# Full-array products for the scores and the edges of an attention, and two copies moved to ScalarE

## The chip, the cores and the metric

The kernel runs on one core of one Trainium2 chip. A core has five engines that run at the same time, each through its own list of instructions in order: TensorE (PE: matrix products; PEld is its weight load), VectorE (DVE), ScalarE (ACT), GpSimd (POOL) and SyncE (SP), which here issues the DMAs. They meet at semaphores only. The metric is the device time in microseconds (us). Lower is better.

## The reference

An attention over 4 batches and 12 heads of 448 rows of 64 numbers, with RMS-normed queries and keys, feeds two expert layers:

```
q_n, k_n = rmsnorm(q, g_q), rmsnorm(k, g_k)
scores = q_n @ k_n.T / sqrt(64); attn = softmax(scores); out = attn @ v
x = out as 1792 x 768
h = x @ w_in;  x = (h * sigmoid(h)) @ w_out              # moe, d_ff 2048
h = x @ w_in;  y = (h * sigmoid(1.702 h)) @ w_out        # moe2
```

All is float32. A float32 operand is kept as two float32r parts, a high part `xh` and a low part `xl = x - xh`, and a product is the sum of three: low by high, high by low, high by high.

## The kernel before

**Attention.** 48 heads are taken as 24 pairs (`NP`). A pair's 448 rows are three chunks of 128 (`NK` = 3) and an edge of 64 rows (`HP`); the edges of the two heads of a pair stand together in one tile of 128 partitions, so a pair has `NG` = 7 groups of rows. On the partitions of `qh`, `ql`, `kh` and `kl` (64 numbers of each head) the first head has 0 to 63 and the second 64 to 127.

What one pair does, by function: `load_qk`, `load_qt`, `load_v` (SP) bring q and k by rows, q already transposed, and v. `square`, `rms_fold`, `polish`, `k_norm` (POOL), `rms_sum` (DVE) and `rms_exp` (ACT) make the norms. `k_T` transposes k on TensorE (L426 for the chunks, `halves` L417 for the edge); `k_hi` (ACT) and `k_lo` (DVE) split it. `q_hi` (DVE, L461) and `q_lo` (POOL, L466) split the transposed q; `v_hi` (DVE, L491) and `v_lo` (POOL, L498) split v. `stack_q` and `stack_k` copy, by DMA, high and low parts on top of each other, so that one product over 128 partitions gives two of the three terms.

`s_mm` makes the scores of one chunk for both heads: the third term, `ql` by `kh`, as two products of 64 partitions, one for each head (L529), then two stacked ones of 128 (L533). The edge of both heads is one group of three products of 128 (L510). The first two pairs take another way (L521). `s_max` (DVE), `s_bias` (POOL) and `s_exp` (ACT) make the softmax. `a_T` transposes the exponentials on TensorE; its last part (m = 6) has the edge's keys (L593, then `halves`). `a_hi` (ACT) and `a_lo` (DVE) split them; `pv` multiplies by v (L631, L624). `recip` (DVE), `r_wide` (ACT), `r_T` (TensorE: L578, `halves`) and `r_copy` (ACT) spread the reciprocal sums, and `x_mul` (DVE) multiplies them in.

`halves` makes the edge's 128 x 64 block into 64 x 64 for each head: two products whose results are 64 partitions high and stand above each other. Each appears as two instructions in the trace.

**Order.** Each step has an offset in `OFF`, in units of an eighth of a pair's turn (`STEP` = 8): `put(STEP * p + OFF[name], ...)`. The tasks are sorted by that number and recorded in that order, so `OFF` alone sets what stands where on each engine. Tiles come from pools with few buffers: four PSUM tiles for scores, two for `a_T`, one for `k_T` and `r_T` together, two buffers for `ql`, `qs`, `ks`, `v`.

From pair 14 on, work for the experts runs in between: `w_conv` turns the 64-bit words of the weights into float32 (ACT, DVE), `w_sum`, `s_hi`, `s_lo` make sums and parts of the weights, and `t_sum`, `t_hi`, `t_lo` sums and parts of the attention's result. All of `t_sum`, `t_lo`, `w_sum` and `s_lo` of this stretch stand on POOL.

**Experts.** 32 units, each seven products of nine instructions (L795, in the order 1, 6, 2, 7, 5, 4, 3), gates, and eight output groups (L904). The first product 4 of a unit waits for a DVE sum (`u`, L888).

Of the kernel before, what the change touches and what calls it, by code (L numbers as in the profile page):

```python
# [75 lines left out]
    "load_qt": -24.5,  # L76
    "load_v": -19.56,
# [4 lines left out]
    "k_norm": -17.87,  # L82
    "k_T": -17.84,
    "k_hi": -16.72,
    "k_lo": -15.3,
    "stack_k": -12.87,
    "q_hi": -17.59,
    "stack_q": -16.68,
    "q_lo": -15.56,
    "v_hi": -6.13,  # L90
    "v_lo": -5.1,
    "s_mm": [-10.89, -7.19, -6.56, -4.96],
    "s_max": [-8.72, -8.6, -6.81, -6.6, -5.38, -4.86, -3.22],
    "s_bias": [-8.32, -6.49, -3.93, -2.94],
    "s_exp": [-7.99, -6.67, -4.87, -3.93, -3.05, -1.3, -1.65],
    "a_T": [-0.76, 1.15, 1.43, 2.5, 3.55, 5.1, 5.94],
    "a_hi": [-0.57, 1.72, 1.87, 4.31, 5.3, 6.24, 7.08],
    "a_lo": [1.02, 2.19, 3.18, 4.6, 5.84, 6.72, 7.86],
    "pv": [2.33, 4.68, 7.7, 9.04],
    "guard": -0.37,  # L100
    "recip": -0.12,
    "r_T": 2.13,
    "r_copy": 3.56,
    "x_mul": 9.46,
    "square": [-24.61, -23.96],
    "lead": [-0.92, 3.78],
    "r_wide": 1.49,
    "w_in": [-51.94, -46.87, -42.73, -40.66, -38.6, -36.0, -33.79, -32.28],
    "w_sum": [-27.36, -26.93, -23.43, -20.47],
    "s_hi": [-30.21, -23.39, -21.4, -18.46],  # L110
    "s_lo": [-28.76, -17.66, -16.28, -14.05],
    "w_out": [-31.16, -25.15, -24.76, -19.09, -18.66, -16.19, -14.68, -10.2],
    "switch": -4.9,
    "t_step": 4.05,
    "t_hi": {1: -79.5, 2: -74.41, 6: -4.77, 7: -1.79, 5: -0.02, 4: 5.6, 3: 5.46},
    "t_lo": {1: -78.66, 2: -72.86, 6: -4.18, 7: 2.3, 5: 2.91, 4: 9.05, 3: 8.34},
    "t_sum": {5: -85.04, 6: -65.06, 7: -56.34, 4: -53.67},
    "second": [-18.32, -15.3, -15.0, -9.57, -14.27, -9.18, -7.33, -6.76],
}
# [3 lines left out]
def kernel(  # L123
# [206 lines left out]
    def attention():  # L330
        st = ExitStack()
        with st:
# [62 lines left out]
            def polish(p):  # L395
                ms, y = rs[p]
                w = sp.tile([128, 2, NG], F32, tag="w", name="w")
# [9 lines left out]
            def k_norm(p):  # L407
                n = raw.pop(p)[:, 1]
                nc.gpsimd.tensor_tensor(
                    n, n,  # L410
                    rs[p][1][:, 1].unsqueeze(2).to_broadcast([128, NG, D]), op=ALU.mult
                )
                kn[p] = n

            def halves(ps, src):
                for i in range(2):
                    nc.tensor.matmul(  # L417
                        ps[64 * i:64 * i + 64, NK * 128:S], src, ident[:, 64 * i:64 * i + 64],
                        start=True, stop=True,
                    )  # L420

            def k_T(p):
                ps = ps_t.tile([128, 512], F32, tag="t", name="t")
                n = kn.pop(p)
                for c in range(NK):
# [4 lines left out]
                halves(ps, n[:, 2 * NK])  # L430
# [48 lines left out]
            def v_parts(t, pad):  # L479
# [7 lines left out]
                return main, t[:, NK * w:]  # L487
# [12 lines left out]
            def s_mm(p, c):  # L500
# [6 lines left out]
                if c == NK:  # L507
                    edge = slice(NK * 128, NK * 128 + 128)
                    for n, (x, y) in enumerate(((1, 0), (0, 1), (0, 0))):
                        nc.tensor.matmul(  # L510
                            ps[0], qq[p][x][:, edge], kk[p][y], start=(n == 0), stop=(n == 2)
                        )
                    return
                chunk = slice(128 * c, 128 * c + 128)
                if p < 2:
                    spans = (((0, 0, S),), ((HP, 0, S - HP), (0, S - HP, HP)))
                    for n, (x, y) in enumerate(((1, 0), (0, 1), (0, 0))):
                        for i in range(2):
                            a = slice(64 * i, 64 * i + 64)
                            for d0, s0, w in spans[i]:  # L520
                                nc.tensor.matmul(  # L521
                                    ps[i][:, d0:d0 + w], qq[p][x][a, chunk],
# [4 lines left out]
                for i in range(2):  # L527
                    a = slice(64 * i, 64 * i + 64)
                    nc.tensor.matmul(  # L529
                        ps[i], qq[p][1][a, chunk], ks[p][a, i], start=True, stop=False  # L530
                    )
                for i in range(2):
                    nc.tensor.matmul(  # L533
                        ps[i], qs[p][:, i, chunk], ks[p][:, i], start=False, stop=True
                    )
# [6 lines left out]
            def s_bias(p, c):  # L542
# [3 lines left out]
                    rr[p][:, 1, g], rr[p][:, 0, g], rs[p][1][:, 0, g], op=ALU.mult  # L546
                )

            def s_exp(p, m):
# [3 lines left out]
                else:  # L553
# [5 lines left out]
                    out=o, in_=sps.pop((p, m)), func=ACTF.Exp, scale=rs[p][1][:, 0, g],  # L559
# [9 lines left out]
            def r_wide(p):  # L569
                rw[p] = ap.tile([128, NG, D], F32, tag="rw", name="rw", bufs=1)  # L570
                nc.scalar.copy(rw[p], rr.pop(p)[:, 3].unsqueeze(2).to_broadcast([128, NG, D]))

            def r_T(p):
                ps = ps_t.tile([128, 512], F32, tag="t", name="t")
                w = rw.pop(p).rearrange("p g d -> p (g d)")
# [3 lines left out]
                halves(ps, w[:, 128 * NK:])  # L579
# [6 lines left out]
            def a_T(p, m):  # L586
# [4 lines left out]
                if m == 2 * NK:  # L591
# [6 lines left out]
                    halves(ps, ec[p][:, NK * 128:])  # L598
# [20 lines left out]
            def pv(p, j):  # L619
                if j == 0:  # L620
                    xps[p] = ps_x.tile([128, S], F32, tag="x", name="x")
                for n, (y, z) in enumerate(((1, 0), (0, 0), (0, 1))):
                    if j == NK:
                        nc.tensor.matmul(  # L624
                            xps[p], vv[p][y][:, 3 * NK * D:], at[p, 2 * NK][z],
# [22 lines left out]
            vbuf = []  # L648
            for i in range(2):
                vbuf.append([  # L650
                    late.tile([128, DM], F32R, tag=f"v{nm}{i}", name=f"v{nm}{i}")[:, :(3 * NK + 2) * D]
                    for nm in "hl"
                ])
                for w in vbuf[i]:
                    nc.gpsimd.memset(f32(w), 0.0)
# [354 lines left out]
```

## Time and profile before

| what | us |
|---|---|
| median of three runs | 1248.39 (1246.15 to 1253.01) |
| the profiled execution's own time | 1250.27 |
| its span, first to last instruction | 1248.5 |
| TensorE busy | 1214.1 (97%) |
| DVE, ACT, POOL busy | 952.0, 659.1, 541.8 |
| attention | up to about 339.5 |
| mean granted TensorE clock | 0.996 |

How to read it: the profile's busy shares are means over the whole span. The attention and the experts load the engines in other ways, so the rows further down are taken from single stretches. A line such as L529 is a line of the kernel before. The granted clock is 1.00 at 2.4 GHz and 0.50 at 1.2 GHz.

### The profile page before, as it was taken

To read this page: it belongs to the slowest core of one execution; us is meant where nothing else is said; L and a number is where in the kernel's file an instruction comes from. 1 tells how busy PE (TensorE), PEld (TensorE's weight loads), DVE (VectorE), ACT (ScalarE), POOL (GpSimd) and SP (SyncE) were. 2 spreads that over 40 slices of the span, in tenths; PEclk is the share of its full clock that TensorE was granted. 3 is DMA by queue.
4 is the path that set the end of the run, shared out by engine and by line. 5 is a ranking of instruction groups with operands and counts; after the bars stand their busy time and mean duration, and the time that the engine had idled before them with its cause. 6 is when DMAs were issued, how large, how long until landed. Compare 5 with 4: busy or idle time off the path is not lost.

```text
span 1248.5 us, 17966 instructions
## 1 busy us (share of the span) xinstructions
PE 1214.1 (97%) x6294; PEld 1059.6 (85%) x6294; DVE 952.0 (76%) x1358; ACT 659.1 (53%) x1270; POOL 541.8 (43%) x677
## 2 busy tenths in 40 slices
PE   5999999999999999999999999899999999999998
PEld 4777777777888888888888888799999989999997
DVE  7888888898678999988788998846666573555563
ACT  4778888877864444454444445553333354333332
POOL 6676679988532224434222332622233242222221
PEclk9999999999999999999999999999999999999999
DMA  4655554465144455533666766122121131111112
GB/s 142 178 147 145 145 150 143 133 198 152 39 152 152 156 182 171 175 114 103 213 228 212 242 225 207 51 89 90 64 74 53 38 129 62 51 51 57 58 38 89
DMA packets 66123, 159.13 MB, mean 127 GB/s; under 512 B 11504, under 2 KB 29424, under 8 KB 66032
## 3 DMA queue, kind: packets, MB, share of 16 engines
q1 hardware_dynamic: 66032, 157.98, 39.9%
q8 instruction: 50, 0.82, 0.3%
q14 instruction: 41, 0.34, 0.1%
HBM read 108.53 MB, written 30.67 MB: 111 GB/s over the span
## 4 chain that ended last, share of the span: by engine, by line
PE 73%; DVE 13%; POOL 5%; issue 3%; ACT 3%; DMA 2%; DVEq 0%; SPq 0%; POOLq 0%; ACTq 0%
PE o L904 33%; PE h L795 23%; PE x L631 5%; PE a L605 3%; PE s L533 2%; DVE ol L285 2%; DVE r L229 2%; PE s L529 1%; POOL gl L812 1%; DVE r L538 1%; POOL acc L316 1%; DVE tl L323 1%; PE t L426 1%; PE a L603 1%; PE x L624 1%
## 5 line engine op out<-in xcount | busy, mean ns | idle before, releaser
L812 POOL TENSOR_TENSOR gl<-g,gh 128x448 fp32r<-128x448 f32 x96 | 118.0, 1229 | 501.4 <-ACT gh L811 500.5
L904 PE MATMUL o<-gl,oh 128*128 128x448 f32 x768 | 282.8, 368 | 3.5 <-POOL gl L812 3.3
L904 PE MATMUL o<-gh,ol 128*128 128x448 f32 x768 | 281.5, 367 | 2.9 <-DVE acc L912 2.5
L904 PE MATMUL o<-gh,oh 128*128 128x448 f32 x768 | 280.6, 365 | 0.0
L795 PE MATMUL h<-th,sl 128*128 128x448 f32 x672 | 175.7, 370 | 5.1 <-DVE u L888 3.8
L795 PE MATMUL h<-tl,sh 128*128 128x448 f32 x672 | 175.1, 369 | 0.0
L795 PE MATMUL h<-th,sh 128*128 128x448 f32 x672 | 174.6, 368 | 0.0
L904 PEld LDWEIGHTS o<-gl,oh 128*128 128x128 f32 x768 | 144.2, 188 | 22.8 <-POOL gl L812 9.5
L904 PEld LDWEIGHTS o<-gh,ol 128*128 128x128 f32 x768 | 144.3, 188 | 17.1 <-DVE acc L912 1.9
L904 PEld LDWEIGHTS o<-gh,oh 128*128 128x128 f32 x768 | 144.2, 188 | 11.6
L916 DVE SCALAR_TENSOR_TENSOR acc<-o,acc 128x896 f32<-128x896 f32 x84 | 91.6, 1091 | 73.8 <-PE o L904 73.6
L795 PEld LDWEIGHTS h<-th,sl 128*128 128x128 f32 x672 | 125.1, 188 | 20.8 <-DVE u L888 8.6
L795 PEld LDWEIGHTS h<-th,sh 128*128 128x128 f32 x672 | 126.7, 189 | 11.9
L795 PEld LDWEIGHTS h<-tl,sh 128*128 128x128 f32 x672 | 126.7, 188 | 11.3
L616 DVE TENSOR_TENSOR al<-a,ah 128x448 fp32r<-128x448 f32 x168 | 103.9, 619 | 36.1 <-ACT ah L612 33.9
L808 ACT ACTIVATE g<-c 128x448 f32<-128x448 f32 x96 | 55.6, 579 | 118.5 <-DVE c L891 117.5
L884 ACT COPY m<-h 128x448 f32<-128x448 f32 x32 | 17.0, 533 | 177.3 <-PE h L795 177.3
L558 ACT ACTIVATE e<-s,r,y 128x448 f32<-128x448 f32 x144 | 104.2, 726 | 10.9 <-POOL r L545 7.1
L612 ACT CAST ah<-a 128x448 fp32r<-128x448 f32 x168 | 87.4, 534 | 42.4 <-PE a L605 29.0
L538 DVE TENSOR_REDUCE r<-s 128x1 f32<-128x448 f32 x168 | 97.5, 614 | 5.7 <-PE s L533 3.7
L912 DVE TENSOR_TENSOR acc<-o,acc 128x896 f32<-128x896 f32 x84 | 90.9, 1083 | 9.0 <-PE o L904 8.9
L888 DVE TENSOR_TENSOR u<-h,m 128x448 f32<-128x448 f32 x64 | 39.8, 622 | 71.6 <-PE h L795 71.0
(135 smaller groups left out, 2206.7 us busy)
## 6 DMA issues: line engine op xcount, KB each, us to landing
d<-w SPq DMA_DIRECT2D x88, 384.0 KB, 3.5
r<-in_moe_w_in SPq DMA_DIRECT2D x32, 768.0 KB, 4.5
r<-in_moe_w_out SPq DMA_DIRECT2D x32, 768.0 KB, 4.7
w<-d SPq DMA_DIRECT2D x32, 384.0 KB, 2.6
w<-r SPq DMA_DIRECT2D x32, 384.0 KB, 3.0
qk<-in_qk SPq DMA_DIRECT2D x22, 448.0 KB, 3.4
qs<-qh SPq DMA_DIRECT2D x88, 96.0 KB, 2.2
qt<-in_q_t SPq DMA_DIRECT2D x24, 256.0 KB, 3.2
```

The lines of the kernel that those rows point to most:

```text
L538: nc.vector.tensor_reduce(rr[p][:, 0, m:m + 1], sps[p, m], axis=AX.X, op=ALU.max, negate=True)
L558: nc.scalar.activation(out=o, in_=sps.pop((p, m)), func=ACTF.Exp, scale=rs[p][1][:, 0, g], bias=rr[p][:, 1, g], accum_out=rr[p][:, 2, g],)
L612: nc.scalar.copy(at[p, m][0], aps[p, m])
L616: nc.vector.tensor_tensor(w, aps.pop((p, m)), f32(at[p, m][0]), op=ALU.subtract)
L631: nc.tensor.matmul(xps[p], vv[p][y][:, c0:c0 + 2 * D], at[p, 2 * j + i][z], start=(j == 0 and n == 0 and i == 0), stop=False,)
L795: nc.tensor.matmul(ps, w[:, c0:c0 + 128], x[:, kk], start=(start and c == 0), stop=(c == 3 * KH - 1), skip_group_check=True,)
L808: nc.scalar.activation(out=g, in_=src, func=ACTF.Silu, scale=(1.0 if first else BETA2))
L812: engine(ENGINE["gate"][key]).tensor_tensor(gl, g, gh.bitcast(F32), op=ALU.subtract)
L888: nc.vector.tensor_tensor(u2 if i == 6 else u3, b, m1, op=ALU.add)
L904: nc.tensor.matmul(o[:, i], x[:, ms], y, start=(t == 0 and c == 0), stop=(t == 1 and c == 2),)
L912: nc.vector.tensor_tensor(a, o, a, op=ALU.add)
L916: nc.vector.scalar_tensor_tensor(a, o, 1.0 / BETA2, a, op0=ALU.mult, op1=ALU.add)
```

## The change

- **Scores.** `q_lo` writes the low part of each head into a tile of its own head, `qlow`, whose other 64 partitions are zero (set once at the start). The third term of the scores then is a product of 128 partitions against the stacked `ks`, as the others. The four products of a chunk go head by head.
- **Edges.** A tile `wide` (128 x 128, zero but for two 64 x 64 blocks) takes the edge's block, written by two DVE copies (`r_edge`, `e_edge`); one product with `twice` (two identities of 64 above each other, in a spare part of a v tile) folds it (`folded`). There is one `wide` for both uses. k's edge is laid out with zeros from the host, so that `k_T` takes it by a fourth transpose; the tiles of the norms have 15 groups for 14.
- **Engines.** `q_hi` and `v_hi` go from DVE to ACT, but for the first pair. Of the three instructions of `q_lo` one is on DVE and two on POOL. Some `t_lo`, `t_sum`, `w_sum`, `s_lo` before the experts go from POOL to DVE.
- **Order.** `OFF` has new numbers throughout; on SP, `load_qk` now stands ahead of `load_v`, and `stack_q` right ahead of `stack_k`.

```diff
     "load_qk": -26.52,
-    "load_qt": -24.5,
+    "load_qt": -20.29,
...
-    "s_mm": [-10.89, -7.19, -6.56, -4.96],
+    "s_mm": [-10.89, -7.63, -6.88, -5.33],
...
+    "hi_on": ["p", "p"],
+    "q_lo_on": ["v", "p", "p"],
+    "edge_on": ["v", "v"],
+    "t_lo_on": {1: "p", 2: "v", 6: "v", 7: "p", 5: "p", 4: "v", 3: "v"},
+    "t_sum_on": {5: "v", 6: "v", 7: "p", 4: "v"},
+    "w_sum_on": ["p", "v", "p", "p"],
+    "s_lo_on": ["v", "v", "v", "p"],
...
-            def halves(ps, src):
-                for i in range(2):
-                    nc.tensor.matmul(
-                        ps[64 * i:64 * i + 64, NK * 128:S], src, ident[:, 64 * i:64 * i + 64],
-                        start=True, stop=True,
-                    )
+            def folded(ps, src):
+                nc.tensor.matmul(ps[:, NK * 128:S], src, f32(twice), start=True, stop=True)
 
             def k_T(p):
...
-                for c in range(NK):
+                for c in range(NK + 1):
                     nc.tensor.transpose(
...
-                halves(ps, n[:, 2 * NK])
...
+            def hi_on(i, p):
+                return nc.scalar.copy if p and OFF["hi_on"][i] == "p" else nc.vector.tensor_copy
+
             def q_hi(p):
                 w = sp.tile([128, NK * 128 + 128], F32R, tag="qh", name="qh")
-                nc.vector.tensor_copy(w, qt[p])
+                hi_on(0, p)(w, qt[p])
                 qq[p] = [w]
...
             def q_lo(p):
-                w = sp.tile([128, NK * 128 + 128], F32R, tag="ql", name="ql")
-                nc.gpsimd.tensor_tensor(w, qt.pop(p), f32(qq[p][0]), op=ALU.subtract)
+                t, h, w = qt.pop(p), qq[p][0], qlow[p % 2]
+                for i in range(2):
+                    a = slice(64 * i, 64 * i + 64)
+                    engine(OFF["q_lo_on"][i]).tensor_tensor(
+                        w[a, i], t[a, :NK * 128], f32(h[a, :NK * 128]), op=ALU.subtract
+                    )
+                w = sp.tile([128, 128], F32R, tag="ql", name="ql")
+                engine(OFF["q_lo_on"][2]).tensor_tensor(
+                    w, t[:, NK * 128:], f32(h[:, NK * 128:]), op=ALU.subtract
+                )
                 qq[p].append(w)
...
                 for o, x in zip(v_parts(vbuf[p % 2][0], True), v_parts(rawv[p], False)):
-                    nc.vector.tensor_copy(o, x)
+                    hi_on(1, p)(o, x)
...
                 for i in range(2):
-                    a = slice(64 * i, 64 * i + 64)
-                    nc.tensor.matmul(
-                        ps[i], qq[p][1][a, chunk], ks[p][a, i], start=True, stop=False
-                    )
-                for i in range(2):
-                    nc.tensor.matmul(
-                        ps[i], qs[p][:, i, chunk], ks[p][:, i], start=False, stop=True
-                    )
+                    for q, z in ((qlow[p % 2], 0), (qs[p], 1)):
+                        nc.tensor.matmul(
+                            ps[i], q[:, i, chunk], ks[p][:, i], start=(z == 0), stop=(z == 1)
+                        )
...
+            def r_edge(p):
+                r = rr[p][:, 3, 2 * NK:]
+                for i in range(2):
+                    a = slice(64 * i, 64 * i + 64)
+                    engine(OFF["edge_on"][0]).tensor_copy(wide[a, a], r[a].to_broadcast([64, D]))
+
+            def e_edge(p):
+                for i in range(2):
+                    a = slice(64 * i, 64 * i + 64)
+                    engine(OFF["edge_on"][1]).tensor_copy(wide[a, a], ec[p][a, NK * 128:])
...
-                halves(ps, w[:, 128 * NK:])
+                folded(ps, wide)
...
-                    halves(ps, ec[p][:, NK * 128:])
+                    folded(ps, wide)
...
+            wide = ap.tile([128, 128], F32, tag="wide", name="wide", bufs=1)
+            nc.gpsimd.memset(wide, 0.0)
+            vbuf, qlow = [], []
             for i in range(2):
+                qlow.append(sp.tile([128, 2, NK * 128], F32R, tag=f"qw{i}", name=f"qw{i}", bufs=1))
+                nc.gpsimd.memset(f32(qlow[i]), 0.0)
...
+            VW = (3 * NK + 2) * D
+            twice = vbuf[0][0][:, VW:VW + D]
+            nc.vector.tensor_tensor(twice, ident[:, :D], ident[:, D:], op=ALU.add)
```

**TensorE, one chunk of scores and the two edge folds behind it, in a pair's turn of the attention.** Before (`s` are scores, `a` and `t` the tiles of transposes, `x` the result):

```order
L605 MATMUL a<-ident,e 128x128 x3
L529 MATMUL s<-ks,ql 128x448 x2
L533 MATMUL s<-ks,qs 128x448 x2
L593 MATMUL a<-ident,e 128x128 x3
L417 MATMUL a<-ident,ec 64x64 x2
L426 MATMUL t<-ident,qk 128x128 x3
L417 MATMUL t<-ident,qk 64x64 x2
L603 MATMUL a<-ident,ec 128x128
```

And of the change at the same place (`qw` is `qlow`, `vh_116` holds `twice`):

```order
L638 MATMUL a<-ident,e 128x128 x3
L553 MATMUL s<-ks,qw_120 128x448
L553 MATMUL s<-ks,qs 128x448
L553 MATMUL s<-ks,qw_120 128x448
L553 MATMUL s<-ks,qs 128x448
L626 MATMUL a<-ident,e 128x128 x3
L433 MATMUL a<-vh_116,wide 128x64
L439 MATMUL t<-ident,qk 128x128 x4
L636 MATMUL a<-ident,ec 128x128
```

The place of the chunk among the transposes is the same; the two products of 64 partitions and the pairs of 64 x 64 are gone, and `k_T` has a fourth transpose.

**ACT, from the exponentials of one chunk to the splits behind `rw`, the same turn.** Before:

```order
L558 ACTIVATE e,r<-s,r,y 128x448
L612 CAST ah<-a 128x448 x2
L558 ACTIVATE ec,r<-s,r,y 128x448
L558 ACTIVATE e,r<-s,r,y 128x448
L612 CAST ah<-a 128x448
L435 ACTIVATE kh<-t,gcol 128x448
L612 CAST ah<-a 128x448
L558 ACTIVATE e,r<-s,r,y 128x448 x2
L571 COPY rw<-r 128x448
L612 CAST ah<-a 128x448 x2
```

And of the change:

```order
L578 ACTIVATE e,r<-s,r,y 128x448
L476 CAST qh<-qt 128x512
L645 CAST ah<-a 128x448
L578 ACTIVATE ec,r<-s,r,y 128x448
L578 ACTIVATE e,r<-s,r,y 128x448
L645 CAST ah<-a 128x448
L447 ACTIVATE kh<-t,gcol 128x448
L645 CAST ah<-a 128x448
L578 ACTIVATE e,r<-s,r,y 128x448 x2
L592 COPY rw<-r 128x384
L516 CAST vh_122<-v 128x3x2x64
L516 CAST vh_122<-v 128x128
```

`qh` stands in front of the `ah` ahead of `ec`, and the two copies of v between `rw` and the last `ah` of the turn.

**DVE, from the attention's last multiplication to the second unit sum of the experts' start.** Before:

```order
L616 TENSOR_TENSOR al<-a,ah 128x448 x6
L639 TENSOR_TENSOR acc<-x,rb 128x2x224
L227 TENSOR_SCALAR r_4489<-r_4489 128x768
L888 TENSOR_TENSOR u_5033<-h,m_5032 128x448
L229 SCALAR_TENSOR_TENSOR r_4489<-r_4489 128x768
L285 TENSOR_TENSOR ol_5064<-d_4486,oh_5063 128x768
L285 TENSOR_TENSOR ol_5049<-d_4699,oh_5048 128x768
```

And of the change:

```order
L332 TENSOR_TENSOR tl_4906<-acc,th_4905 128x448
L672 TENSOR_TENSOR acc<-x,rb 128x2x224
L332 TENSOR_TENSOR tl_4906<-acc,th_4905 128x448 x2
L332 TENSOR_TENSOR tl_4904<-acc,th_4903 128x448 x3
L236 TENSOR_SCALAR r_4561<-r_4561 128x768
L928 TENSOR_TENSOR u_5112<-h,m_5111 128x448
L238 SCALAR_TENSOR_TENSOR r_4561<-r_4561 128x768
```

Five low parts `tl` that POOL made before now stand on DVE between the last `acc` and the first `u`.

## Rows read from the trace of the kernel before

**Rows 1.** Stretches: us, busy us (x) of PE, PEld, DVE, ACT, POOL, PEclk, DMA.
```profile
33.18:199.65 166.47, 166.47 (x1056) 131.38 (x1055) 143.85 (x272) 135.02 (x337) 117.71 (x236) 1.00 0.54 154
199.65:332.05 132.40, 127.93 (x785) 98.89 (x784) 115.17 (x210) 108.82 (x266) 106.23 (x180) 0.99 0.51 143
350.80:354.30 3.50, 3.16 (x9) 2.81 (x10) 2.73 (x4) 1.15 (x2) 1.19 (x1) 0.51 0.86 290
```

**Rows 2.** Timeline of PE, one turn: start us, us, instruction, xcount.
```profile
100.47 0.49 PE L605 MATMUL a<-ident,e 128*128 128x128 f32 x3
100.71 0.65 PE L631 MATMUL x<-ah,vl 128*128 128x448 f32 x2
101.20 0.58 PE L631 MATMUL x<-ah,vh 128*128 128x448 f32 x2
...
102.01 0.27 PE L601 MATMUL a<-swap,ec 128*128 128x128 f32 x1
102.12 0.49 PE L605 MATMUL a<-ident,e 128*128 128x128 f32 x3
102.54 0.47 PE L529 MATMUL s<-ks,ql 64*128 64x448 f32 x2
102.94 0.68 PE L533 MATMUL s<-ks,qs 128*128 128x448 f32 x2
103.45 0.49 PE L593 MATMUL a<-ident,e 128*128 128x128 f32 x3
103.87 0.34 PE L417 MATMUL a<-ident,ec 128*64 128x64 f32 x4
104.14 0.55 PE L426 MATMUL t<-ident,qk 128*128 128x128 f32 x3
...
105.05 0.49 PE L605 MATMUL a<-ident,e 128*128 128x128 f32 x3
...
110.09 0.49 PE L578 MATMUL t<-ident,rw 128*128 128x128 f32 x3
...
111.29 0.56 PE L631 MATMUL x<-ah,vh 128*128 128x448 f32 x2
```

**Rows 3.** ACT groups by line: shapes, count, busy us, mean ns, idle before.
```profile
L281 ACT CAST oh<-d 128x768 fp32r<-128x768 f32 x60 | 47.0, 834 | 0.0
...
L571 ACT COPY rw<-r 128x448 f32<-128x448 f32 x24 | 13.6, 565 | 0.0
```

**Rows 4.** DVE groups by line.
```profile
L323 DVE TENSOR_TENSOR tl<-acc,th 128x448 fp32r<-128x448 f32 x45 | 33.8, 783 | 2.6 <-ACT th L319 2.6
...
L461 DVE CAST qh<-qt 128x512 fp32r<-128x512 f32 x24 | 19.6, 819 | 0.0
...
L491 DVE CAST vh<-v 128x384 fp32r<-128x384 f32 x24 | 13.0, 541 | 0.0
...
L491 DVE CAST vh<-v 128x128 fp32r<-128x128 f32 x24 | 6.1, 254 | 0.0
```

**Rows 5.** Timeline of SP, the same turn: issues of the stacked copies.
```profile
103.19 2.40 SPq L473 DMA_DIRECT2D qs<-qh  x4
...
108.74 1.24 SPq L453 DMA_DIRECT2D ks<-kl  x2
```

**Rows 6.** Page, DMA issues: KB each, median us from issue to landing.
```profile
qs<-qh SPq DMA_DIRECT2D x88, 96.0 KB, 2.2
```

**Rows 7.** Timeline of PE, first unit of the experts: idle time and releaser in brackets.
```profile
351.14 1.49 PE L795 MATMUL h<-th,sl 128*128 128x448 f32 x3 [2.23 <-DVE u L888]
```

**Rows 8.** Timeline of DVE, the same unit.
```profile
343.48 0.62 DVE L888 TENSOR_TENSOR u<-h,m 128x448 f32<-128x448 f32 x1 [2.52 <-PE h L795]
...
344.94 3.74 DVE L285 TENSOR_TENSOR ol<-d,oh 128x768 fp32r<-128x768 f32 x2
```

**Rows 9.** Chain of waits, second unit, the same two instructions: start us, us, what.
```profile
376.30 1.82 DVE ol L285 x2
```

**Rows 10.** POOL group by line: the zeros at the start.
```profile
L655 POOL MEMSET vh<- 128x704 f32 x2 | 1.4, 684 | 0.0
```

More of the change, by code (lines that the diff above doesn't have):

```diff
@@ L81 @@
     "polish": -18.96,
-    "k_norm": -17.87,
-    "k_T": -17.84,
+    "k_norm": -18.36,
+    "k_T": -17.01,
     "k_hi": -16.72,
[L85 to L91, printed above, removed]
-    "s_mm": [-10.89, -7.19, -6.56, -4.96],
[L93 to L96, printed above, removed]
@@ L100 @@
+    "a_T": [-0.76, 1.11, 1.58, 2.5, 3.79, 5.04, 6.02],
+    "a_hi": [-0.05, 1.72, 2.0, 4.31, 4.76, 6.24, 7.08],
+    "a_lo": [1.02, 2.09, 2.57, 4.52, 5.89, 6.98, 7.86],
+    "pv": [2.33, 4.68, 7.27, 9.04],
     "guard": -0.37,
-    "recip": -0.12,
+    "recip": -0.17,
+    "r_edge": 0.91,
+    "e_edge": 2.32,
     "r_T": 2.13,
-    "r_copy": 3.56,
+    "r_copy": 2.53,
     "x_mul": 9.46,
-    "square": [-24.61, -23.96],
+    "square": [-24.61, -23.52],
     "lead": [-0.92, 3.78],
     "r_wide": 1.49,
-    "w_in": [-51.94, -46.87, -42.73, -40.66, -38.6, -36.0, -33.79, -32.28],
@@ L109 @@
[L109 to L112, printed above, removed]
+    "w_in": [-54.21, -48.34, -42.73, -40.66, -37.35, -36.1, -33.13, -32.28],
+    "w_sum": [-28.11, -27.53, -23.43, -20.47],
+    "s_hi": [-29.75, -22.67, -21.4, -15.51],
+    "s_lo": [-11.15, -18.03, -16.28, -14.15],
+    "w_out": [-31.44, -25.15, -24.76, -19.09, -18.66, -16.19, -14.68, -7.22],
@@ L520, in s_mm @@
                             for d0, s0, w in spans[i]:
+                                q = qlow[p % 2][:, i] if x else qq[p][0]
                                 nc.tensor.matmul(
-                                    ps[i][:, d0:d0 + w], qq[p][x][a, chunk],
+                                    ps[i][:, d0:d0 + w], q[a, chunk],
                                     kk[p][y][a, s0:s0 + w], start=(n == 0 and s0 == 0),
@@ L679, in n_polish @@
             def n_polish(p, i):
-                ms, y, w = (t[:, i] for t in rs[p])
+                ms, y, w = (t[:, PART[i]] for t in rs[p])
                 nc.vector.tensor_scalar(
@@ L727, in attention @@
             prep = (load_qt, k_T, k_hi, k_lo, q_hi, q_lo)
-            for fn in stats + prep + (load_v, v_hi, v_lo, guard, recip, r_wide, r_T, r_copy, x_mul):
+            for fn in stats + prep + (load_v, v_hi, v_lo, guard, recip, r_wide, r_edge, e_edge, r_T, r_copy, x_mul):
                 p0 = 2 if fn in stats or fn is load_qt else 1 if fn in prep or fn is load_v else 0
@@ L973, in layout @@
         main, edge = rows(t)
-        qk += [main, edge.reshape(main.shape[0], 128, -1)]
+        if t is q:
+            edge = edge.reshape(main.shape[0], 128, -1)
+        else:
+            n, _, e, d = edge.shape
+            pad = np.zeros((n, 128, 2 * d), k.dtype)
+            pad[:, :e] = edge.transpose(0, 2, 1, 3).reshape(n, e, 2 * d)
+            edge = pad
+        qk += [main, edge]
     arrays["in_qk"] = np.concatenate(qk, axis=2)
```

102 lines of the change are left out of this document (55 added, 47 removed).

## The prediction

> **What bounds the kernel now.** I read the stretches first. From 33.18 to 199.65 us, thirteen pairs' turns of 12.8 us (from one pair's `r_T` to the next), TensorE is busy 166.47 of 166.47 us at full clock [rows 1]: it waits for nobody, and a turn is as long as its instructions. DVE is busy 143.85 of it, ACT 135.02, POOL 117.71, which is 11.07, 10.39 and 9.05 us a turn. From 199.65 to 332.05, the last ten turns and a bit, where the experts' weights are made ready as well, TensorE is busy 127.93 of 132.40, and DVE 115.17, ACT 108.82, POOL 106.23 [rows 1]: nobody is free. The reader is to see that the first stretch answers to TensorE alone and the second to several engines. Then I read one turn of TensorE start by start [rows 2], since its busy time doesn't show what one instruction costs the next. Products of experts, over two thirds of the span, are not touched.
>
> **TensorE, the scores.** A chunk now: from the start of three transposes at 102.12 to the next transposes at 103.45, 1.33 us [rows 2]. In it the two products of 64 partitions start 0.42 after the transposes and hold the array 0.40 until the stacked ones start (102.54 to 102.94). Full products of the same length: 101.20 to 102.01 is 0.81 for four, and 100.47 to 102.01 is 1.54 for three transposes and six. So three transposes and four full products take 1.54 - 0.405 = 1.135, and a chunk saves 0.19; three chunks a turn, 0.57 (I take the chunk that stands behind products as the other two).
>
> The Trainium skill ("TensorE: Matmul & The Clock Gate", Part 3) says that products on different rows of the array run side by side in the time of one, which speaks against this change: two of 64 partitions would cost 0.20, and four full ones would be 0.2 longer. The trace agrees that the two run together (one row, 0.47 for both [rows 2]), not that they take the time of one: until the next can start it is 0.40, that of two full products. By that rule the 0.40 would be something else than array time, and might stay.
>
> **TensorE, the edges.** From 103.45 to 105.05 stand seven transposes and two foldings, 1.60 us [rows 2]. A transpose in a row costs 0.11 (102.01 to 102.12). Of the change there are eight transposes and one `folded`: 0.88 and its cost. That one is not in the trace: it can't be under two passes of 64 columns at the transposes' pace, 0.11, nor over what the pair costs now, 0.27 (103.87 to 104.14); I take 0.20, nearer to the measured pair than to the transposes, since it is of the pair's kind. Saved: 1.60 - 1.08 = 0.52. `r_T` with two products: 1.20 now (110.09 to 111.29), 0.73 without a folding (100.47 to 101.20), so 0.93 with it: 0.27 saved. In all 0.57 + 0.52 + 0.27 = 1.36 a turn (1.22 to 1.54), and TensorE's turn goes from 12.8 to 11.45.
>
> **ACT.** It gets `qh` (512 columns) and `vh` (384 and 128), and `rw` is 64 columns shorter. A copy from SBUF of 448 columns takes 0.565, of 768 0.834 [rows 3], 0.84 ns a column; so 0.62 + 0.51 + 0.30 - 0.05 = 1.38 a turn. End to end ACT would have 10.39 + 1.38 = 11.77 of work, more than TensorE's 11.45; adjacent instructions overlap somewhat, which makes it less. In the order both copies stand in front of an `ah`, which TensorE (two PSUM tiles for `a_T`) and `al` on DVE wait for. Between 11.45 and 11.77 plus waits I take 11.7 for the turn: ACT and TensorE nearly level. The first stretch saves 13 x 1.1 = 14.3 us (0 if the turn stays, 17.7 if TensorE alone counts).
>
> **DVE and POOL.** DVE loses `qh` (0.82) and `vh` (0.54 + 0.25) [rows 4], 1.61 a turn. It gains a third of `q_lo`: 384 columns from SBUF, by `tl` (0.78 for 448 [rows 4]) 0.67; and four copies of 64 x 64, each between nothing and the 0.25 of 128 x 128; I take 0.13. So 1.61 - 1.19 = 0.4 less, and 10.7 a turn: hidden in the first stretch. POOL's norm tiles are larger by 15 groups to 14, at most 0.65 on its 9.05, and `q_lo` is two instructions there for one: in a turn of 11.7 it has 2.6 us free, which hides both. The new wait: `e_edge` on DVE must find that `folded` of `r_T` has read `wide`; behind it stands the next `al`, for which `pv` waits. In the order TensorE has `r_T` ahead of that `pv`, so the wait is over first; I cost it at nothing, and at one `folded`, 0.2 a turn, if not.
>
> On SP the loads are moved, and the four copies `qs` stand right ahead of `ks`. Now they issue at 103.19 for 2.40 us, the last `ks` at 109.98 [rows 5], landing 2.2 later [rows 6], at 112.2; the first use is a turn after 102.54, at 115.3. The slack of 3.1 shrinks by the shorter turn to about 2, so this costs nothing.
>
> **The second stretch.** DVE there: less 8 x 0.82 and 10 x 0.80, 14.6; more 9 thirds of `q_lo` at 0.67 (6.0), 40 edge copies at 0.13 (5.2; 0 to 10), and what comes from POOL in this stretch by the order: seven `t_sum` and four `t_lo` at 0.78 (8.6), three `s_lo` of 768 columns (an estimate by columns: 1.34 each, 4.0) and one `w_sum` (0.7). Sum: +9.9, and 115.17 becomes 125.1. TensorE alone would need 127.93 - 10.35 x 1.36 = 113.9. So DVE is what is late next; with 2% idle 128, which saves 4.4 us. The bounds: 0, or 18.5 if the edge copies are free and DVE's instructions are shorter with a less busy POOL.
>
> **The border to the experts.** TensorE waits 2.23 us for `u` at 351.14 [rows 7], and in the 3.5 us around it the granted clock is 0.51 [rows 1], the lower level of 1.2 GHz, which loses another 1.7. In front of that `u` DVE has two `ol` that take 3.74 beside POOL's run of `tl` [rows 8], and 1.82 a unit later [rows 9]. The change halves POOL's run, but puts five `tl` on DVE, 3.9 us, of which the 2.52 that DVE waits for TensorE [rows 8] hide most. So `u` comes 3.74 - 1.82 less 1.4, 0.5 us earlier at least; whether the clock then stays up is open. I take 2 of the 3.9 (0 to 3.9). At the start POOL also writes the zeros of two `qlow` of 768 columns; 704 take 0.68 [rows 10], so 1.5 and, with the rest, 1.9 us more ahead of its first square, which waits for a load anyway: between 0 and 1.9, I take 0.3 lost.
>
> **Sum.** 14.3 + 4.4 + 2.0 - 0.3 = 20.4 us less than the profiled execution's 1250.27, 1229.9. The median of three runs, 1248.39, is 1.9 below that execution: 1228.
>
> **Rivals.**
> - *TensorE stays the only bound.* ACT's and DVE's overlaps leave room everywhere: 17.7 + 14.1 + 3.9 = 35.7, or 1213. For it: TensorE never waited in the first stretch, and the new order may be as well packed. Against: 11.77 of ACT's work in 11.45.
> - *The second stretch and half the first are lost.* ACT's waits make the turn 12.3 (6.5 us saved) and DVE's work from POOL eats all the rest: 1242. For it: 125 of DVE's work in 132.
> - *The 0.40 isn't array time.* Scores save nothing, TensorE's turn is 12.0: 13 x 0.8 = 10.4, 2 and 2 behind it: 1234. Against: two starts 0.40 apart for two products of 0.20 each is what plain sharing gives. This is the rule of the Trainium skill named above.
> - *Slower: ACT's idle time stays.* ACT idles 12.8 - 10.39 = 2.4 us a turn, all of it waits for others in a fixed order. If these stay in place and the copies come on top, the turn is 12.8 + 1.4 = 14.2, and 23 turns lose some 32 us: 1280; with half of them filled 14 us are lost, 1262. It decides from the point where over 1.0 us of ACT's idle remains a turn (12.8 - 11.77). Against: the copies stand in front of an `ah`, where ACT waits for TensorE's transposes, which now come sooner.
>
> **How the numbers follow.** Forecast 0.60 (its own range 1220 to 1237), TensorE alone 0.13, half lost 0.16, not array time 0.05, slower 0.06. Within 0.5% is about what a measurement here can tell from no change: 1242.2 to 1254.6. Of half lost, about a third falls in there, and of the slower case little: same 0.07, slower 0.05, faster 0.88. The range of 8 in 10 reaches from TensorE alone to half lost: 1212 to 1241.
>
> **What would show it.** Right: in the new profile no instruction of 64 partitions but in the first two pairs, turns of 11.5 to 12.0 with ACT over 95% busy and TensorE with short waits for `ah` or `al`; DVE over 94% in the ten turns before the experts. A turn under 11.45 would say that I have overpriced `folded`; 12.0 with TensorE full would say that the 0.40 stayed; turns over 12.8 with ACT waiting would make the forecast wrong, as would waits on `wide` ahead of `folded`, or a DMA on the stacked tiles.

## The result, and the profile after

The changed kernel takes 1263.08 us (median of 4 runs, 1261.97 to 1264.37) beside 1247.62 for the kernel before in the same rounds: a ratio of 1.0116 [1.0084, 1.0149]. It is 1.2% slower, where 1228 was forecast. The profiled execution has a span of 1260.7 us at a mean granted clock of 0.995.

The stretches of [rows 1], from the 1st `r_T` to the 14th and from there to the last, first of the kernel after, then of experiment 1 below, in which the four small edge copies are on POOL and nothing else differs (columns as in [rows 1]):

```profile
32.76:203.67 170.91, 154.56 (x964) 139.19 (x963) 154.28 (x301) 148.60 (x378) 119.73 (x247) 1.00 0.56 153
203.67:348.61 144.94, 124.04 (x724) 106.81 (x723) 135.13 (x251) 119.87 (x294) 99.75 (x175) 0.96 0.47 132
```

```profile
34.58:186.21 151.63, 150.79 (x963) 139.35 (x963) 133.50 (x247) 145.67 (x378) 132.50 (x298) 1.00 0.63 171
186.21:319.20 132.99, 120.06 (x723) 104.63 (x722) 118.36 (x209) 118.62 (x294) 108.37 (x213) 0.99 0.51 144
```

The reader is to see DVE, the third pair of numbers: 154.28 us for thirteen turns, 11.87 a turn, where 10.7 was forecast, and 135.13 in the last ten, where 125.1 was. TensorE's busy time did fall (166.47 before), but it now has 16.35 us of idle time in a stretch in which it had none. Against the kernel before, in us:

| part | forecast | after | experiment 1 |
|---|---|---|---|
| up to the first `r_T` (33.18 before) | +0.3 | -0.4 | +1.4 |
| thirteen turns (166.47) | -14.3 | +4.4 | -14.8 |
| last ten turns (132.40) | -4.4 | +12.5 | +0.6 |
| border and experts (from the last `r_T`) | -2.0 | -4.4 | -2.0 |
| span | -20.4 | +12.2 | -14.8 |

(The parts are rounded one by one.) A turn named below is the commonest of the first thirteen: 12.79 before, 13.13 after.

What TensorE waits for after the change, in the thirteen turns (us in total, times, longest):

```profile
PE x L664 <- DVE acc L672: 10.1, 12, 0.9
PE t L439 <- POOL qk L424: 5.6, 13, 0.5
```

Both are late for one reason, which a stretch of one turn shows. DVE after the change, and POOL at the same time:

```profile
120.78 0.68 DVE L452 SCALAR_TENSOR_TENSOR kl<-t,gcol,kh 128x448 fp32r<-128x448 f32 x1
121.37 1.18 DVE L598 COPY wide<-r 64x64 f32<-64x64 f32 x2
122.58 0.62 DVE L649 TENSOR_TENSOR al<-a,ah 128x448 fp32r<-128x448 f32 x1
123.12 0.61 DVE L558 TENSOR_REDUCE r<-s 128x1 f32<-128x448 f32 x1
123.65 0.97 DVE L485 TENSOR_TENSOR qw<-qt,qh 64x384 fp32r<-64x384 f32 x1
124.55 0.61 DVE L558 TENSOR_REDUCE r<-s 128x1 f32<-128x448 f32 x1
125.08 0.60 DVE L672 TENSOR_TENSOR acc<-x,rb 128x448 f32<-128x448 f32 x1
```

```profile
121.48 1.01 POOL L485 TENSOR_TENSOR qw<-qt,qh 64x384 fp32r<-64x384 f32 x1
122.58 0.46 POOL L489 TENSOR_TENSOR ql<-qt,qh 128x128 fp32r<-128x128 f32 x1
122.99 1.22 POOL L392 TENSOR_TENSOR sq<-sq 128x480 f32<-128x480 f32 x1
125.24 0.20 POOL L565 TENSOR_TENSOR r<-r,y 128x2 f32<-128x2 f32 x1 [1.03 <-DVE r L558]
```

The two copies of `r_edge`, 64 columns each, occupy DVE from 121.37 to 122.55. POOL's `q_lo` starts at 121.48 and ends at 122.49: the copies are over 0.06 later. DVE's own third of `q_lo` starts at 123.65, beside POOL's fold, which ends at 124.21, and takes 0.97. Behind them in DVE's queue stand the maxima `r`, for which POOL waits (1.03 in the last row) with `polish` and `k_norm` queued behind it, and `acc`, for which TensorE waits. The durations of one line (min/median/max in ns, first and last start) say how common that is; after, three lines:

```profile
L598 DVE COPY wide<-r x48: 173/192/999, 29.7 to 347.2; 64x64 f32<-64x64 f32 x48
L603 DVE COPY wide<-ec x48: 172/191/1053, 34.4 to 349.8; 64x64 f32<-64x64 f32 x48
L485 DVE TENSOR_TENSOR qw<-qt,qh x24: 538/966/976, 9.4 to 324.4; 64x384 fp32r<-64x384 f32 x24
```

and of the kernel before the copy `qh`, of which the mean of 819 in [rows 4] was all that was read:

```profile
L461 DVE CAST qh<-qt x24: 415/923/1190, 7.5 to 301.9; 128x512 fp32r<-128x512 f32 x24
```

A copy has a length of its own and another beside POOL, and 819 was the mean over the two. Instance by instance it is a rule: of the 96 edge copies 61 take 0.195 us or less, and the 35 that take over 0.25 all end 46 to 63 ns behind the end of a POOL instruction; of DVE's 24 thirds of `q_lo`, the 20 that take over 0.75 all end 409 to 416 ns behind POOL's fold. The groups by line give 25.8 us for the 48 copies of `r_edge` and 13.7 for those of `e_edge`: 1.65 us a turn, not 0.52.

The other lines that answer to those before. TensorE, a chunk of scores and the edges, to be compared with [rows 2]:

```profile
116.73 0.49 PE L638 MATMUL a<-ident,e 128*128 128x128 f32 x3
116.97 0.45 PE L553 MATMUL s<-ks,qw 128*128 128x448 f32 x1
117.26 0.37 PE L553 MATMUL s<-ks,qs 128*128 128x448 f32 x1
117.47 0.37 PE L553 MATMUL s<-ks,qw 128*128 128x448 f32 x1
117.67 0.37 PE L553 MATMUL s<-ks,qs 128*128 128x448 f32 x1
117.87 0.49 PE L626 MATMUL a<-ident,e 128*128 128x128 f32 x3
118.20 0.33 PE L433 MATMUL a<-vh,wide 128*128 128x64 f32 x2
118.96 0.66 PE L439 MATMUL t<-ident,qk 128*128 128x128 f32 x4 [0.43 <-POOL qk L424]
```

A chunk is 116.73 to 117.87, 1.14 us, where 1.135 was worked out from 1.33. ACT's copies, to be compared with [rows 3] (busy us, mean ns):

```profile
L476 ACT CAST qh<-qt 128x512 fp32r<-128x512 f32 x23 | 14.3, 622 | 0.0
L592 ACT COPY rw<-r 128x384 f32<-128x384 f32 x24 | 12.4, 515 | 0.0
L516 ACT CAST vh<-v 128x384 fp32r<-128x384 f32 x23 | 12.1, 527 | 0.0
L516 ACT CAST vh<-v 128x128 fp32r<-128x128 f32 x23 | 7.1, 310 | 0.0
```

These are the forecast's 0.62, 0.51 and 0.30. The stacked copies [rows 5] issue at 117.48 and 123.27 in this turn and land in the same 2.2 us [rows 6]; TensorE never waited for them. At the border to the experts, [rows 7 to 9], DVE makes the five `tl` ahead of the first `u`:

```profile
356.64 3.13 DVE L332 TENSOR_TENSOR tl<-acc,th 128x448 fp32r<-128x448 f32 x5
...
360.16 0.61 DVE L928 TENSOR_TENSOR u<-h,m 128x448 f32<-128x448 f32 x1
...
361.56 1.81 DVE L294 TENSOR_TENSOR ol<-d,oh 128x768 fp32r<-128x768 f32 x2
```

The two `ol` take 1.81 (3.74 before) with POOL idle beside them, TensorE waits 0.56 for the second `u` at 365.84 (2.23 before), and the granted clock there is 1.00 (0.51 before).

### The profile page after: what moved, and what is told of

It reads as the page before. It is cut to its first block, busy times and chain, and to the rows that moved or that the text cites. A ratio compares the mean times of both kernels' runs of the same rounds, so it can differ in the third digit from the quotient of the medians.

```text
span 1260.7 us, 17842 instructions
## 1 busy us (share of the span) xinstructions
PE 1192.6 (95%) x6126; PEld 1073.3 (85%) x6126; DVE 986.3 (78%) x1435; ACT 683.3 (54%) x1339; POOL 528.1 (42%) x679
## 4 chain that ended last, share of the span: by engine, by line
PE 60%; DVE 21%; POOL 7%; issue 5%; ACT 5%; DMA 1%; SPq 0%; DVEq 0%; ACTq 0%; POOLq 0%
PE o L944 34%; PE h L835 23%; DVE r L558 3%; DVE al L649 3%; DVE ol L294 2%; DVE wide L598 2%; POOL gl L852 1%; DVE r L238 1%; DVE tl L332 1%; ACT e L578 1%; DVE acc L672 1%; ACT ah L645 1%; PE x L664 1%; DVE ms L398 1%; POOL acc L325 1%
## 5 line engine op out<-in xcount | busy, mean ns | idle before, releaser
L835 PEld LDWEIGHTS h<-th,sh 128*128 128x128 f32 x672 | 126.4, 188 | 11.5
```

The lines of the kernel that those rows point to most:

```text
L835: nc.tensor.matmul(ps, w[:, c0:c0 + 128], x[:, kk], start=(start and c == 0), stop=(c == 3 * KH - 1), skip_group_check=True,)
```

## The experiments

**Theories,** by the names that the expectations use. S: DVE's SBUF copies and its third of `q_lo` wait for the POOL instruction that is running, and that, not TensorE's or ACT's work, makes the turn. A, the slower rival of the prediction: ACT has too much, and its copies come on top of its idle time. O: the order on POOL makes the turn, where `polish` and `k_norm` stand behind an `s_bias` that waits for DVE. N: each of DVE's instructions counts alike, whatever POOL does. Two more that no expectation names: C, the products of 64 partitions gave nothing back; D, `q_lo` on DVE by itself is what costs.

**1. The four edge copies on POOL.**

```
-    "edge_on": ["v", "v"],
+    "edge_on": ["p", "p"],
```

> The changed kernel with the four edge copies of a turn (r_edge, e_edge) on POOL instead of DVE. Theory S (DVE's copies out of SBUF wait until the POOL instruction that is running has ended; DVE's row of instructions, 11.8 us a turn, with POOL and ACT closes a loop of 13.13 us): DVE loses 1.6 us a turn, POOL gains about 1.0, the turn goes to 12.0 to 12.4 and the time to 1240 to 1250. Rival A (the two copies on ACT set the turn): the turn stays at 13.1 and the time at 1263. Rival O (the order on POOL: polish and k_norm stand behind an s_bias that waits for DVE): about 13.0, TensorE's wait for k_norm stays at 0.4 a turn or grows, 1260.

1234.88 us, ratio 0.9883 [0.9856, 0.9909]: more than I expected of S, and neither A's 13.1 nor O's 13.0 came. Ten of the thirteen turns are 11.46 to 11.51, three are longer (12.47, 12.41, 11.96; mean of all 11.66), and TensorE is busy 150.79 of 151.63 (shown above): it is the bound again, in the ten at the 11.45 that the forecast gave it. So 28 us of the changed kernel hang on four copies a turn, and no version found was faster. In their place on POOL the copies take 0.23 in the median:

```profile
L598 POOL COPY wide<-r x48: 228/234/1058, 29.6 to 317.6; 64x64 f32<-64x64 f32 x48
```

**2. All of `q_lo` on POOL** (D).

```
-    "q_lo_on": ["v", "p", "p"],
+    "q_lo_on": ["p", "p", "p"],
```

> The changed kernel with all three instructions of q_lo on POOL. Theory S: DVE loses 0.97 us a turn, POOL gains 1.04; the second r_edge copy still waits behind a POOL q_lo, so the turn goes only to 12.3 to 12.8, the time to 1248 to 1257. Rival A: 1263. Rival O: POOL has more work in front of k_norm, so no gain or slower, 1263 to 1270.

1260.73, ratio 1.0087 [1.0065, 1.011]; turns of 12.85, a miss: S had 12.3 to 12.8. With `q_lo` off DVE 0.3 us a turn comes back in the first stretch, but the copies, which nothing touched, got longer beside the longer `q_lo` on POOL: 31.9 us for `r_edge` and 21.2 for `e_edge`, for 25.8 and 13.7. So this run doesn't measure D alone. Experiment 1 does: there the third of `q_lo` stays on DVE (median 0.80), and the turn comes back. D is out as the main cause.

**3. The two copies of ACT back on DVE** (A).

```
-    "hi_on": ["p", "p"],
+    "hi_on": ["v", "v"],
```

> The changed kernel with q_hi and v_hi back on DVE, all else as changed. Rival A: ACT falls from 11.4 to 10.1 us a turn and the turn to about 12.2, 1243. Theory S: DVE gets 1.4 to 1.9 us more a turn (the q copy beside POOL takes 0.92), the turn goes to 14.3 to 15, the time to 1285 to 1300.

1287.53, ratio 1.0296 [1.0276, 1.0316]; turns of 14.25. A would have made it faster. TensorE's waits are those for DVE and for POOL behind it, only larger:

```profile
PE x L664 <- DVE acc L672: 19.2, 20, 1.3
PE t L439 <- POOL qk L424: 17.4, 21, 2.2
PE a L636 <- DVE al L649: 10.9, 19, 1.3
```

**4. The kernel before with the scores alone as full-array products** (C); `q_lo` is three instructions on POOL, and the order is that of before. The edit in `s_mm`, without the tiles and `q_lo`:

```
...
-                    nc.tensor.matmul(
-                        ps[i], qq[p][1][a, chunk], ks[p][a, i], start=True, stop=False
-                    )
...
+                    for q, z in ((qlow[p % 2], 0), (qs[p], 1)):
...
```

> The kernel before with only the scores by full-array products (zero-padded low parts, q_lo as three instructions on POOL, all else and the order as before). If the two products of 64 partitions cost two full ones and the drain: TensorE's turn 12.8 - 0.57 = 12.23, no wait, and 1238 to 1242. If the 0.40 us is not array time: turn 12.8, 1248. If POOL's longer q_lo (2.5 us instead of 1.3) delays k_norm or s_bias: 12.4 to 12.8.

1258.67, ratio 1.0069 [1.0049, 1.0089], a miss: I expected 1238 to 1242. Its first stretch is TensorE's, with turns of 12.41, 0.38 shorter than before. A chunk takes 1.15 there (115.19 to 116.34 in its timeline), so three save 0.54, near the forecast's 0.57, and one transposed `ec` starts 0.16 late in the turn. C is out. What was gained is lost behind it: the last ten turns, from 197.07 to 339.01, take 141.94, 9.5 longer than before, with POOL, which has the longer `q_lo`, busy 118.04 in them (106.23 before). That POOL is the cause was not tried. The rows are its first twelve turns and the eleven behind them:

```profile
35.21:184.10 148.89, 148.50 (x972) 126.84 (x971) 137.23 (x250) 122.04 (x312) 117.57 (x239) 1.00 0.57 159
184.10:339.00 154.90, 140.61 (x869) 115.81 (x868) 127.64 (x233) 119.62 (x295) 130.19 (x220) 0.98 0.47 135
```

**5 and 6. One pair of copies on POOL, the other on DVE.** In 5 `r_edge` is on POOL, in 6 `e_edge`:

```
-    "edge_on": ["v", "v"],
+    "edge_on": ["p", "v"],      # 5
+    "edge_on": ["v", "p"],      # 6
```

> The changed kernel with only r_edge on POOL, e_edge left on DVE. Theory S: nearly all of the cost is r_edge, whose second copy (0.97 us) waits for POOL's q_lo; e_edge mostly runs free (0.18 each). So the first stretch's turn is TensorE's, 11.5 to 11.7, and the time 1230 to 1238. If instead the number of DVE's instructions counts (rival N: four copies, each alike), half of the 28 us that all four gave come back: about 1249.

> The changed kernel with only e_edge on POOL, r_edge left on DVE. Theory S: the wait of r_edge's second copy stays in the loop; the turn is 13.13 less the 0.43 of e_edge, 12.6 to 12.8, the time 1250 to 1258. Rival N: about 1249, as the run with r_edge alone on POOL.

5: 1245.38, ratio 0.9979 [0.9969, 0.9988], turns of 12.41: slower than I expected. 6: 1252.94, ratio 1.0036 [1.0022, 1.0049], turns of 12.71, as expected. N, by which both would take about 1249, is out: the two intervals lie apart. In 5 the copies of `e_edge`, of 0.17 to 0.19 in most turns after the change, have become long, with nothing done to them:

```profile
L603 DVE COPY wide<-ec x48: 175/412/947, 35.8 to 334.1; 64x64 f32<-64x64 f32 x48
```

DVE reaches them earlier now against POOL's `vl`, and falls beside it; DVE first, then POOL:

```profile
110.53 1.00 DVE L603 COPY wide<-ec 64x64 f32<-64x64 f32 x2
111.57 0.62 DVE L649 TENSOR_TENSOR al<-a,ah 128x448 fp32r<-128x448 f32 x1
```

```profile
110.04 1.45 POOL L523 TENSOR_TENSOR vl<-v,vh 128x384 fp32r<-128x384 f32 x2
```

`vl` ends at 111.49, the copies at 111.53. So which of the copies is dear isn't theirs: it is what POOL does when DVE comes to them.

**7. The same bytes written by another form of instruction,** a reduction over one element, still on DVE.

```
-    engine(OFF["edge_on"][0]).tensor_copy(wide[a, a], r[a].to_broadcast([64, D]))
+    nc.vector.tensor_reduce(
+        wide[a, a], r[a].to_broadcast([64, D]).unsqueeze(2), axis=AX.X, op=ALU.add
+    )
```

(and so for `e_edge`)

> The changed kernel with the four edge copies still on DVE at the same places, but written as sums over one element (tensor_reduce), an instruction that in the trace of before takes its 0.61 for 448 elements beside any POOL instruction. Theory S: no copy waits for POOL, each takes 0.15 to 0.2, DVE falls from 11.8 to about 10.9 a turn, the turn to 11.5 to 11.9; POOL isn't loaded as in the run with all edges on POOL, so the second stretch gains too: 1224 to 1236. If any DVE instruction of this place waits (for a semaphore, for its operands): the second r_edge still takes 0.97 and the time is 1263.

1240.4, ratio 0.9942 [0.9925, 0.9959]; I expected 1224 to 1236. This is the sharpest of the runs: same engine, same place in the order, same bytes, and the wait is gone.

```profile
L598 DVE TENSOR_REDUCE wide<-r x48: 198/210/220, 29.7 to 322.7; 64x64 f32<-64x64 f32 x48
```

No reduction of the 48 takes over 220 ns, where copies took up to 999; those of `e_edge` take 198 to 219. Of the 96, 51 start with over 0.25 us of a POOL instruction still to run. That is the part of S on copies by itself. The turn is 12.05, 0.6 over TensorE's; what TensorE waits for is POOL's `k_norm`:

```profile
PE t L439 <- POOL qk L424: 10.4, 18, 1.6
```

Some of that may be the same wait, turned around. DVE's third of `q_lo` now mostly comes first (median 0.54, 0.97 after), and it is POOL's fold behind it that gets longer; after the change, then here:

```profile
L392 POOL TENSOR_TENSOR sq<-sq x22: 1192/1218/1236, 18.9 to 310.5; 128x480 f32<-128x480 f32 x22
```

```profile
L392 POOL TENSOR_TENSOR sq<-sq x22: 1197/1552/1593, 18.9 to 287.6; 128x480 f32<-128x480 f32 x22
```

**8. Edges on POOL, the two copies on DVE.**

```
-    "hi_on": ["p", "p"],
+    "hi_on": ["v", "v"],
...
-    "edge_on": ["v", "v"],
+    "edge_on": ["p", "p"],
```

> All four edge copies on POOL, and q_hi and v_hi back on DVE: what the two copies on ACT are worth once the edges are off DVE. Theory S: DVE goes from 10.05 to about 11.6 a turn and more where the q copy waits for POOL (0.92), the turn to 12.0 to 12.6, the time to 1243 to 1255, against 1235 with the copies on ACT. If ACT at 96% holds back the turn: under 1235.

1247.6, ratio 0.9996 [0.9982, 1.0009]; turns of 12.16. Beside experiment 1 this is 12.7 us longer, which is what moving `qh` and `vh` to ACT is worth: the reverse of A.

**9 to 11. `polish` earlier on POOL, and the sum `twice` later at the start,** with the edges as reductions (9), on POOL (10), and `r_edge` as a reduction with `e_edge` on POOL (11).

```
-    "polish": -18.96,
+    "polish": -20.1,
...
-            nc.vector.tensor_tensor(twice, ident[:, :D], ident[:, D:], op=ALU.add)
...
                 n_norm(0, nc.vector)
+                nc.vector.tensor_tensor(twice, ident[:, :D], ident[:, D:], op=ALU.add)
                 k_T(0)
```

> Edges by one-element reductions on DVE as in e7, and two moves: `polish` on POOL comes ahead of the `s_bias` that waits for DVE's maximum, and the sum `twice` at the start comes behind the first normalisation. If what is left of e7's turn over TensorE's 11.46 is the wait for `k_norm` (10.4 us in 18 waits there), the turn goes from 12.05 to 11.5 to 11.8 and the start gets some 1.4 us shorter: 1229 to 1236. If that `s_bias`, now about 0.6 us later, is what ACT and `al` wait for, the turn stays at 12.0 to 12.3 and the time at 1238 to 1243.

> Edges on POOL as in e1, and the same two moves. The first stretch of e1 is bound by TensorE (11.46 a turn), so the earlier `polish` can give little there: two turns of 12.4 in it, 1.9 us. The start gives some 1.4 us. In the ten turns before the experts POOL was busy 13.0 of 14.0 us, and less waiting behind `s_bias` may give 0 to 4. So 1229 to 1233; at 1235 or more the order on POOL has nothing to give once the copies are off DVE.

> As e9, but the two copies of `e_edge` are on POOL: DVE has two reductions of 0.21 us a turn less, POOL two copies of 0.24 more. If TensorE is the bound already, the first stretch stays at 11.5 to 11.8 a turn, and only the ten turns before the experts tell: 1228 to 1234 if DVE is what is late there, 1234 to 1240 if POOL is.

9: 1238.75, ratio 0.9915 [0.9897, 0.9933]. The turn falls to 11.5 to 11.6 as expected, 5.2 us in the thirteen turns beside experiment 7, but the last ten turns take 137.4, which is 3.4 more than there, and the first `r_T` comes 2.6 later. 10: 1252.86, ratio 1.0031 [1.0021, 1.0042], and 11: 1253.04, 1.0035 [1.0022, 1.0049], were misses: turns of 12.26 and 12.13. As I read the waits, where POOL also has copies `polish` holds its `s_bias` back, ACT's exponentials come late for it (10.9 us of waits in the thirteen turns of 10), and POOL idles for them in its turn; 10:

```profile
113.85 0.94 POOL L388 TENSOR_TENSOR sq<-qk 128x448 f32<-128x448 f32 x1
116.04 0.25 POOL L584 TENSOR_SCALAR r<-r 128x7 f32<-128x7 f32 x1 [1.25 <-ACT e L578]
```

The start got no shorter by moving `twice` (TensorE's first wait stays 9.1 us, 7.7 before).

**12. Edges on POOL** as in experiment 1, **and `s_bias` on DVE.**

```
-                eng = nc.vector if p == 0 else nc.gpsimd
-                eng.tensor_tensor(
-                    rr[p][:, 1, g], rr[p][:, 0, g], rs[p][1][:, g], op=ALU.mult
+                nc.vector.scalar_tensor_tensor(
+                    rr[p][:, 1, g], rr[p][:, 0, g], 1.0, rs[p][1][:, g], op0=ALU.mult, op1=ALU.mult
                 )
```

> Edges on POOL as in e1; the four `s_bias` of a pair on DVE, as scalar_tensor_tensor of one or two columns, where they stand right behind their maximum. In e1's ten turns before the experts POOL waits 7.8 us for DVE's maxima with `polish` and `k_norm` queued behind, TensorE 6.6 us for `k_norm`, ACT 6.3 us for POOL's `s_bias`. If POOL's place in the order is what keeps this stretch as long as before, it gets 5 to 10 us shorter, the first stretch stays at 11.46 a turn (DVE 10.0 + 4 x 0.17): 1225 to 1231. If DVE is late there, or if its short products wait for POOL's instruction as its copies do (up to 0.8 each), the turn of the first stretch grows to 12 or more, or the last ten turns stay at 133: 1235 to 1250.

1238.66, ratio 0.9917 [0.9901, 0.9934]: not better than experiment 1 (the intervals overlap). The wait for `k_norm` has shrunk to 0.9 us in 2 times, and the last ten turns take 134.5 us all the same; ACT waits 7.2 us for DVE's `s_bias` there. Products of one or two columns can wait for POOL as well:

```profile
L564 DVE SCALAR_TENSOR_TENSOR r<-r,y x96: 141/162/1051, 16.8 to 317.8; 128x2 f32<-128x2 f32 x72, 128x1 f32<-128x1 f32 x24
```

## Why the prediction was wrong

The step that failed stands under "DVE and POOL": "four copies of 64 x 64, each between nothing and the 0.25 of 128 x 128; I take 0.13", with the third of `q_lo` at 0.67, "so ... 10.7 a turn: hidden in the first stretch". The copies measured 1.65 a turn and not 0.52, the third of `q_lo` 0.88 (1.55 and 0.97 in the first stretch), and DVE 11.87. That is less than the turn of 13.13, so DVE isn't full. But what it waits for waits for it: `s_bias` on POOL needs its maxima, `polish` and `k_norm` are queued behind, ACT needs `s_bias`, and DVE's `al` needs ACT. A delay in the middle of the queue goes around this loop and lengthens the turn: the chain of waits through the turn shown above runs over DVE to 115.7, over POOL to 117.9, over ACT to 119.9, and by POOL back to DVE, where the two copies of `r_edge` stand in it from 121.37 to 122.55. The bound of 0.25 was taken from a row of another shape whose mean hid two kinds (18 of 24 took 208 to 219 ns, the others 258 to 583), and the upper end of a copy in these turns is the rest of whatever POOL is running, about one of its instructions, 1.0 us. So it isn't true of time that the engines "meet at semaphores only": in experiment 7 place, data and order are the same, and only the form of the instruction takes the wait away.

- *TensorE.* Right: a turn of 11.45 forecast, 11.46 in most turns of experiment 1. The chunk's 1.14 rules out the rival in which the scores save nothing. But the 0.19 lies at the two changes of shape and not in the pair: behind products the kernel before has 0.50, 0.39 and 0.52 from start to start (106.19, 106.69, 107.08, 107.60), and experiment 1 has 0.40, 0.40 and 0.41 (113.32, 113.72, 114.12, 114.53). That the two products of 64 partitions run together isn't shown by their standing in one row, as the timeline puts all neighbours of one kind in a row; it is by the mean of one, 467 ns, beside 0.47 for the pair.
- *ACT.* Right in its durations; 11.77 was too much: in experiment 1 it is busy 145.67 of 151.63, 11.2 a turn, and TensorE waits 0.8 us in the whole stretch, none of it for ACT. The mean turn there, 11.66, is near the 11.7 forecast by luck: ten turns are TensorE's alone, and three are longer, one of them with a wait of 0.55 for DVE.
- *The slower rival* gave 1262, next to the measured 1263, but by the wrong mechanism: ACT's copies are a gain (experiments 3 and 8).
- *The second stretch.* The same failed term: 18.0 us for the 40 copies (5.2 forecast), 135.13 of DVE (125.1 forecast). Without it these turns are back at 133 (experiment 1), so the 12.5 lost there is nearly all of this cause. The forecast gain of 4.4 didn't come in any run. In experiment 1 no engine is busy over 91% there, and the remedies for the wait for `k_norm` (9, 10, 12) each turned it into another; what sets this stretch is left open. Part of its loss after the change may be the granted clock: 0.96, with three stretches of 4.3 us in which it averages 0.60, so mostly the lower level of 1.2 GHz, where there was one before.
- *The border.* Right in its mechanism (both the wait for `u` and the lower clock went), and past its bounds: 4.4, with 2.0 taken from 0 to 3.9. Experiment 1, with the same code there, has 2.0.
- *The start.* The first `r_T` was 0.4 earlier instead of 0.3 later, but the first wait of TensorE grew by 1.4, of the same kind: DVE's first instructions end only when POOL's zeros [rows 10] are written, at 5.51 (0.74 each for 768 columns, 0.68 for 704 before, and six of them for four).

```profile
1.32 4.27 DVE L973 COPY swap<-ident 128x64 f32<-128x64 f32 x2 [1.32 <-POOL ident masks.py:199]
2.82 2.77 DVE L694 TENSOR_TENSOR vh<-ident 128x64 fp32r<-128x64 f32 x1
3.67 1.92 DVE L743 TENSOR_TENSOR gcol<-gcol 128x1 f32<-128x1 f32 x1
```

```profile
4.09 0.74 POOL L691 MEMSET vh<- 128x768 f32 x1
4.77 0.74 POOL L691 MEMSET vl<- 128x768 f32 x1
```

The row L743 is a product of one column that takes 1.92 us. The two copies of L973 last over all six of POOL's zeros, one behind the other. That it is these zeros was not tried apart.

What the rows show is that copies end some 50 ns behind POOL's instruction, and that products with both inputs in SBUF get longer beside it (0.97 for 0.54, over 0.41 behind the fold's end), while reductions and the products `al` that read PSUM (168 of 572 to 627 ns) don't. The Trainium skill has this as a rule ("SBUF — State Buffer", section "Who interferes with whom"): VectorE's second pair of SBUF ports is also GpSimd's, it is held by one of the two for a whole instruction while the other stands still, and on this chip copies can want it, as can products of two SBUF tensors, but reductions never. The trace agrees on copies (173 to 999 ns for one shape), on reductions (198 to 220), and on products (141 to 1051). By that rule POOL's zeros, which read nothing, would not hold the product L743; in the rows it ends with them, behind copies that were held, and which of the two it waited for no run here shows apart.

## What to carry to other kernels

Before an instruction is moved to DVE, look at its form and at what POOL runs at that moment: a small copy can cost the rest of a POOL instruction, here five times its own length, and a reduction over one element that writes the same bytes cost its own length in all 96 instances. Look at POOL's durations too, since a product of DVE that comes first can lengthen POOL's. Read the smallest, the median and the largest duration of a line before taking its mean as a price or as a bound. And an engine that isn't full can still set the turn, when what it waits for is waiting for it: hidden work is hidden only outside such a loop.

## What was not expected of the hardware

That a mere change of form, copy to reduction, takes 22.7 us off 1263.08 (experiment 7), the two measured apart against the same kernel before at ratios of 1.0116 [1.0084, 1.0149] and 0.9942 [0.9925, 0.9959]. And that making DVE's queue shorter can make its copies dearer: in experiment 5 the same copies went from a median of 191 ns to 412, since they came earlier and met POOL's `vl` with more of it still to run (0.96 at 110.53 in the rows of 5; 0.10 at 113.56 after the change).
